# Ordering every engine's stream by hand in an attention + ReGLU-FFN kernel on one core

## The chip, the cores and the metric

The kernel runs on one core of one Trainium2 chip. The metric is device time in microseconds (us), taken as the median of several executions; lower is better. A profile of one execution is there for every kernel. Its span, from the first to the last instruction, is about 2 us shorter than the device time (420.0 against 421.8 for the kernel before), so differences are what is compared between the two.

The engines are called as in the profile: PE (TensorE, matmuls), PEld (its weight loads), DVE (VectorE), ACT (ScalarE), POOL (GpSimd), SP (SyncE, which here only issues DMAs). "L214" is line 214 of a kernel; the two kernels have different line numbers for the same code.

## The reference

Causal attention by blocks of 64, then a gated FFN on the concatenated heads:

```python
# q, k, v: (8, 8, 576, 64) fp32, normal * 0.1   -> B, H, S, D
scores = (1 / sqrt(64)) * (q @ k^T)                 # (B, H, 576, 576)
scores = where(pos // 64 >= pos' // 64, scores, -1e9)
attn   = softmax(scores)                            # (+1e-9 in the denominator)
x      = (attn @ v).transpose(0, 2, 1, 3).reshape(4608, 512)
gate   = max(x @ w_gate, 0)                         # w_gate, w_val: (512, 1536)
out    = (gate * (x @ w_val)) @ w_out               # w_out: (1536, 512), out fp32
```

## The kernel before

The work is cut into 32 head pairs, r = 4 b + hp: four pairs for each of the 8 batches. A pair needs scores (q k^T), an exp on ACT, zeros written over the 64x64 blocks that the mask removes from the diagonal ("corner memsets"), two attention-value products (one for each head), a division by the row sum, and a transpose of the result into xT. The FFN of batch b needs the xT of all four of its pairs. FFN matmuls come out of one generator, and `ffn(n)` emits the next n of them between the steps of the attention of later batches, so that PE has something to do while ACT and DVE work on the attention.

Only PE was ordered by hand. On the other engines a scheduler chose the order. The parts that the change touches (cut):

```python
    def new_stage(w):                       # fp32 landing buffers: 5, used over again
        return sb.tile([128, 2048], FP, name="stage", bufs=5)[:, 0:w]

    def early_load(b, per, gate=None):      # batches 0, 1, 2: load fp32, cast on DVE
        ...
            for t in range(2):
                nc.vector.tensor_copy(m[t][:, :, 64 * h0 : 64 * h1]..., sts[t]...)   # L125
        ...
    def load_batch(b):                      # batches 3 to 7: casting loads on POOL's queue,
        for t, src in enumerate((q, k, v)): # each followed at once by its transposing DMA
            ...                             #   nc.gpsimd.dma_start(dst, src...)       L162
            if t < 2:
                nc.sync.dma_start_transpose(qTm or kTm, m[t])                        # L167
                nc.sync.dma_start_transpose(qTt or kTt, tl[t])

    def scores_1(r):
        sc = scores(b, hp, [(0, 0, True)])
        nc.scalar.activation(at[:, :, 0:512], sc, AF.Exp, scale=scale)
        nc.vector.memset(at[64:128, :, 0:64], 0.0)          # a corner
        sc = scores(b, hp, [(0, 1, True), (384, 3, True)])
        nc.scalar.activation(at[:, :, 512:1024], sc, AF.Exp, scale=scale)
        nc.vector.memset(...); nc.vector.memset(...)        # two more corners
    ...
    with tc.manual_schedule(engines={mybir.EngineType.PE}):
        pe_transposes(0, 0, *early[0])
        for r in range(4):                  # batch 0: nothing to overlap with
            scores_1(r)
            if r < 3:
                pe_transposes(0, r + 1, *early[0])
            if r > 0:
                head_av(r - 1, 0)
            scores_2(r)
            ...
        *early[1], marks1 = early_load(1, 4, w_in)     # waits until the last weight landed
        ...
        ffn(76)
        for r in range(4, 4 * B):
            b, hp = divmod(r, 4)
            a = {1: [2, 2, 4, 6], 2: [4, 4, 4, 12]}.get(b, [8, 4, 8, 16])
            ...
            scores_1(r)
            ffn(a[0])
            if r > 4:
                head_av(r - 1, 0)
                ffn(a[1])
                head_av(r - 1, 1)
                to_xT_pe(r - 1) if r <= 8 else to_xT_dma(r - 1)   # shortened
            ...
            elif hp == 0 and b + 1 < B:
                load_batch(b + 1)
            ffn(a[2])
            scores_2(r)
            scores_3(r)
            ...
            ffn(a[3])
```

The whole kernel before:

The softmax here doesn't subtract the row's maximum and nothing guards it: scores larger than these inputs give would overflow.

## Time and profile before

The median is 421.8 us beside the changed kernel (421.29 to 423.13, 4 runs). What matters, by stretch of the profiled 420.0 us:

| stretch | us | what limits it |
|---|---|---|
| batch 0, up to the first FFN matmul | 0 to 47.7 | serial chain of one pair's attention, at a half-speed PE |
| rest of FFN 0, batch 1, batch 2 (pairs 4 to 11) | 47.7 to 137.7 | mixture: PE busy 67.3 of the 80 us from 60 to 140 |
| batches 3 to 7 | 137.7 to 339 | PE, 40.25 us a batch |
| last pair's end and last FFN parts | to 420 | PE |

From the page of the kernel before: the span, busy tenths of PE in 40 slices of 10.5 us each, the granted PE clock in tenths of full speed, and the shares of the chain of waits.

```profile
span 420.0 us, 7452 instructions
...
PE   2672796887899999999999999999999999999995
...
PEclk9955599999999999999999999999999999999999
...
PE 75%; DMA 7%; DVE 6%; issue 5%; ACT 4%; SPq 2%; POOL 1%; ACTq 0%; DVEq 0%
```

PE is at 9 tenths or more from the 12th slice on and has holes before it; slices 1 and 4 are the worst. The chain of waits, too, runs through PE for 75% of the span. What is to be gained by order therefore lies at the front.

The table by stretch of the kernel before. Its columns are the stretch, its length, then busy us (and instruction counts) of PE, PEld, DVE, ACT and POOL, the granted clock, the mean share of DMA engines in use and GB/s.

```profile
60.00:140.00 80.00, 67.31 (x637) 33.55 (x647) 46.91 (x132) 35.95 (x51) 29.33 (x35) 1.00 1.46 134
140.00:340.00 200.00, 195.80 (x1654) 93.78 (x1684) 88.87 (x241) 93.06 (x139) 33.54 (x40) 1.00 0.76 88
```

In 200 us of steady batches PE stands for 4.2 us, so that 0.84 us of a 40.25 us batch is not PE work.

The timeline of PE before: start, duration, engine, line, operation, result<-operands, tile shapes, count, and in brackets the idle time before the instruction with what ended it.

```profile
4.13 0.61 PE L195 MATMUL ffnp<-ident,q_bf 128*128 128x128 bf16 x4 [4.13 <-DVE q_bf L125]
...
42.20 0.61 PE L293 MATMUL ffnp<-ident,xnat 128*128 128x128 bf16 x4 [8.18 <-DVE xnat L276]
...
47.66 1.49 PE L316 MATMUL ffnp<-xT,wg_75 128*128 128x512 bf16 x3 [0.33 <-issue]
...
68.89 0.40 PE L195 MATMUL ffnp<-ident,k_bf 128*128 128x128 bf16 x4
```

Two things are to be seen. Four 128-wide transposes take 0.61 us at 4 and at 42 us and 0.40 at 69 us: PE runs cold at the front. And PE stands for 8.18 us before 42.20, waiting for a division on DVE. The timeline of DVE says what DVE did in that time:

```profile
39.30 0.69 DVE L125 CAST q_bf<-stage 128x1024 bf16<-128x1024 f32 x1 [6.25 <-DMA stage<-in_q_dram]
...
41.66 0.48 DVE L276 TENSOR_TENSOR xnat<-av,recip 128x320 bf16<-128x320 f32 x1
```

It had been given a cast of batch 1 to do first, and stood 6.25 us for the data of it. The PE part of the table of waits before (total us, times, longest) has this as its largest line:

```profile
PE ffnp L293 <- DVE xnat L276: 13.9, 8, 8.2
```

### The profile page before, as it was taken

The page shows a single profiled execution, that of the slowest core. Times are in us where ns is not written, and L with a number is a line of the kernel's source. Part 1 is how long each engine was busy: PE and PEld are TensorE (multiplying, and loading weights), DVE is VectorE, ACT ScalarE, POOL GpSimd, SP SyncE. Part 2 cuts the span into 40 slices and gives each one's busy share as a digit, 9 for nine tenths or more (in the row PEclk, how much of TensorE's full clock was granted, in tenths as well). Part 3 has the DMA queues.
Part 4 walks back from the last instruction along what each step waited for, and adds up shares of the span by engine and source line. Part 5 has one row for each costly group of instructions (what it writes and reads, how often), then busy time and mean ns, then how long its engine had stood idle before and what let it go on. Part 6 is the DMA issues. An engine that isn't in the chain of part 4 may idle for free.

```text
span 420.0 us, 7452 instructions
## 1 busy us (share of the span) xinstructions
PE 373.0 (89%) x2941; PEld 181.5 (43%) x2992; DVE 192.9 (46%) x503; ACT 161.7 (39%) x237; POOL 73.4 (17%) x98
## 2 busy tenths in 40 slices
PE   2672796887899999999999999999999999999995
PEld 1441443444444444444444444444444444444442
DVE  4742456755565444443444444444434442433331
ACT  1532033443445435544553455245425521321320
POOL 2500200034737370065003000300000000000000
PEclk9955599999999999999999999999999999999999
DMA  8998989239999999299539304920021002002004
GB/s 205 186 203 181 232 149 275 36 47 167 166 126 124 146 195 112 44 149 188 63 71 130 112 16 83 164 68 14 16 91 48 19 19 100 0 2 100 2 1 99
DMA packets 144274, 43.54 MB, mean 104 GB/s; under 512 B 127856, under 2 KB 139632, under 8 KB 144240
## 3 DMA queue, kind: packets, MB, share of 16 engines
q0 software_dynamic: 76128, 13.57, 48.2%
q1 hardware_dynamic: 68112, 29.51, 32.5%
q8 instruction: 23, 0.38, 0.4%
q14 instruction: 11, 0.09, 0.1%
HBM read 37.75 MB, written 9.44 MB: 112 GB/s over the span
## 4 chain that ended last, share of the span: by engine, by line
PE 75%; DMA 7%; DVE 6%; issue 5%; ACT 4%; SPq 2%; POOL 1%; ACTq 0%; DVEq 0%
PE ffnp L344 22%; PE ffnp L328 20%; PE ffnp L316 19%; PE av L266 6%; PE sc L214 6%; DMA wv_82<-in_moe_w_val_dram 3%; DVE xnat L276 2%; DMA stage<-in_v_dram 2%; DMA stage<-in_k_dram 1%; PE ffnp L195 1%; ACT attnT_95 L232 1%; ACT gate_sb L325 1%; ACT attnT_95 L229 1%; DVE recip L275 1%; SPq L133 1%
## 5 line engine op out<-in xcount | busy, mean ns | idle before, releaser
L325 ACT ACTIVATE gate_sb<-ffnp 128x512 bf16<-128x512 f32 x108 | 64.5, 597 | 136.6 <-PE ffnp L316 134.3
L338 DVE TENSOR_TENSOR hT<-gate_sb,ffnp 128x512 bf16<-128x512 bf16 x108 | 74.3, 688 | 70.7 <-PE ffnp L328 68.9
L344 PEld LDWEIGHTS <-hT 128*128 128x128 bf16 x432 | 39.1, 98 | 43.5 <-issue 1.7
L354 DVE COPY ob<-ffnp 128x512 f32<-128x512 f32 x36 | 24.9, 692 | 56.5 <-PE ffnp L344 53.8
L344 PE MATMUL ffnp<-wo_84,hT 128*128 128x512 bf16 x141 | 36.6, 379 | 0.2
L344 PE MATMUL ffnp<-wo_85,hT 128*128 128x512 bf16 x138 | 36.1, 380 | 0.4
L344 PE MATMUL ffnp<-wo_83,hT 128*128 128x512 bf16 x136 | 35.8, 380 | 0.4
L276 DVE TENSOR_TENSOR xnat<-av,recip 128x320 bf16<-128x320 f32 x64 | 31.5, 491 | 2.2
L162 POOL DMA_DIRECT2D q_bf<-in_q_dram x20 | 17.6, 894 | 82.9 <-PE ffnp L198 44.9
L240 ACT ACTIVATE attnT_95<-sc 128x1024 bf16<-128x1024 f32 x16 | 16.4, 1022 | 33.0 <-PE sc L214 33.0
L240 ACT ACTIVATE attnT_94<-sc 128x1024 bf16<-128x1024 f32 x16 | 16.4, 1024 | 31.5 <-PE sc L214 31.5
L316 PE MATMUL ffnp<-xT,wg_77 128*128 128x512 bf16 x95 | 24.6, 380 | 2.2 <-DVE hT L338 2.1
L266 PEld LDWEIGHTS <-attnT_94 128*128 128x128 bf16 x480 | 18.5, 101 | 18.5 <-DVE xnat L276 14.8
L316 PE MATMUL ffnp<-xT,wg_75 128*128 128x512 bf16 x94 | 25.6, 394 | 0.4 <-issue 0.3
L328 PE MATMUL ffnp<-xT,wv_79 128*128 128x512 bf16 x90 | 25.3, 391 | 0.3
L316 PE MATMUL ffnp<-xT,wg_78 128*128 128x512 bf16 x96 | 24.8, 379 | 0.4 <-DVE qTt_91 L203 0.4
L266 PEld LDWEIGHTS <-attnT_95 128*128 128x128 bf16 x480 | 18.8, 102 | 14.5 <-DVE xnat L276 11.0
L328 PE MATMUL ffnp<-xT,wv_82 128*128 128x512 bf16 x87 | 24.2, 380 | 0.6 <-issue 0.2
L229 ACT ACTIVATE attnT_95<-sc 128x1024 bf16<-128x1024 f32 x16 | 16.4, 1023 | 21.7 <-PE sc L214 21.7
L316 PE MATMUL ffnp<-xT,wg_76 128*128 128x512 bf16 x94 | 24.6, 380 | 0.1
L328 PE MATMUL ffnp<-xT,wv_81 128*128 128x512 bf16 x89 | 24.4, 380 | 0.4
L328 PE MATMUL ffnp<-xT,wv_80 128*128 128x512 bf16 x91 | 24.4, 379 | 0.3
(109 smaller groups left out, 433.5 us busy)
## 6 DMA issues: line engine op xcount, KB each, us to landing
out_dram<-ob SPq DMA_DIRECT2D x32, 256.0 KB, 2.8
stage<-in_v_dram SPq DMA_DIRECT2D x27, 128.0 KB, 4.9
q_bf<-in_q_dram POOLq DMA_DIRECT2D x20, 128.0 KB, 5.8
k_bf<-in_k_dram POOLq DMA_DIRECT2D x20, 128.0 KB, 7.2
stage<-in_q_dram SPq DMA_DIRECT2D x4, 512.0 KB, 4.4
stage<-in_k_dram SPq DMA_DIRECT2D x4, 512.0 KB, 5.5
v_bf_97<-in_v_dram POOLq DMA_DIRECT2D x12, 128.0 KB, 8.0
stage<-in_q_dram SPq DMA_DIRECT2D x4, 256.0 KB, 3.6
```

The lines of the kernel that those rows point to most:

```text
L162: nc.gpsimd.dma_start(dst, src[b, :, 128 * c : 128 * c + n, :].rearrange("h p d -> p h d"),)
L214: nc.tensor.matmul(o, kTm[b % 2][ps, c, hp, :] if c < 4 else kTt[b % 2][ps, hp : hp + 2, :].rearrange("p h n -> p (h n)"), qTm[b % 2][ps, ...
L229: nc.scalar.activation(at[:, :, 0:512], sc, AF.Exp, scale=scale)
L240: nc.scalar.activation(at[:, :, 1024:1536], sc, AF.Exp, scale=scale)
L266: nc.tensor.matmul(av[:, p, :], at[:, hh, col : col + 128], vb[:, c, h, :], start=(p == 0), stop=(c == p), skip_group_check=True,)
L276: nc.vector.tensor_tensor(out=xnat[:, :, 64 * hh : 64 * hh + 64], in0=av[:, :, 0:64], in1=recip.to_broadcast([128, NCH, 64]), op=AX.mult,)
L316: nc.tensor.matmul(gate, wg[i][:, c, fo : fo + 128], x[:, c, :], start=(c == 0), stop=(c == 3),)
L325: nc.scalar.activation(gate_sb, gate, AF.Relu)
L328: nc.tensor.matmul(val, wv[i][:, c, fo : fo + 128], x[:, c, :], start=(c == 0), stop=(c == 3),)
L338: nc.vector.tensor_tensor(out=h, in0=gate_sb, in1=val, op=AX.mult)
L344: nc.tensor.matmul(op, hT[f][:, 128 * s : 128 * (s + 1)], wo[f // 4][:, f % 4, :], start=(f == 0), stop=(f == 11),)
L354: nc.vector.tensor_copy(ob, op)
```

## The change

The intent: take order away from the scheduler on all five engines. Nothing is meant to be computed differently. (1) Landing buffers become ten of half the size, so that no load of batch 0 has to wait until a cast frees one; its casts are spread over DVE, ACT and POOL. (2) Junk matmuls on zeros warm PE and keep it warm. (3) The casts of batch 1 move behind 64 FFN matmuls. (4) Corner memsets move out of the score functions to one place per pair, after the pair's last FFN group, and the second exp goes behind an FFN group; the sizes of the groups change. (5) Since SP is now in program order, the loads of batch b+1 (on POOL's queue) and their transposing DMAs are emitted apart: loads at the first pair of a batch, transposes at the third. Besides, copies of transposed outputs go from DVE to ACT, in batch 0 the second head gets another buffer in PSUM (the memory that matmuls write to), and some memsets of the start go to POOL. The core of the diff (cut, and in parts shortened):

```diff
     def new_stage(w):
-        return sb.tile([128, 2048], FP, name="stage", bufs=5)[:, 0:w]
+        return sb.tile([128, 1024], FP, name="stage", bufs=10)[:, 0:w]
 ...
+    def dma_transposes(b):          # was inside load_batch, right behind the loads
+        for t in range(2):
+            nc.sync.dma_start_transpose((qTm, kTm)[t][b % 2]..., m[t]...)      # L189
+            nc.sync.dma_start_transpose((qTt, kTt)[t][b % 2][:, 0:4, :], tl[t])
 ...
     def scores_1(r):
         nc.scalar.activation(at[:, :, 0:512], sc, AF.Exp, scale=scale)
-        nc.vector.memset(at[64:128, :, 0:64], 0.0)
         sc = scores(b, hp, [(0, 1, True), (384, 3, True)])
-        nc.scalar.activation(at[:, :, 512:1024], sc, AF.Exp, scale=scale)
-        nc.vector.memset(at[64:128, :, 512:576], 0.0)
-        nc.vector.memset(at[64:128, :, 896:960], 0.0)
+        return lambda: nc.scalar.activation(at[:, :, 512:1024], sc, AF.Exp, scale=scale)
 ...
+    def corners(r, eng):
+        for c in (0, 512, 896, 1024):
+            eng.memset(at[64:128, :, c : c + 64], 0.0)
 ...
-        av = psum_av.tile([128, NCH, 65], FP, name="av")
+        if b == 0 and hh == 1:
+            av = psum_ffn.tile([128, NCH, 65], FP, name="ffnp")
+        else:
+            av = psum_av.tile([128, NCH, 65], FP, name="av")
 ...
-        nc.vector.tensor_copy(xT_of(b)[:, hp, :], br[:, 0:512])
+        nc.scalar.copy(xT_of(b)[:, hp, :], br[:, 0:512])
 ...
+    def junk(n):
+        jp = psum_ffn.tile([128, 512], FP, name="ffnp")
+        for _ in range(n):
+            nc.tensor.matmul(jp, ident, zeros, start=True, stop=True)
 ...
-    with tc.manual_schedule(engines={mybir.EngineType.PE}):
+    with tc.manual_schedule(engines={E.PE, E.DVE, E.Activation, E.Pool, E.SP}):
+        ... e0.load(h0) for batch 0; junk(12); casts and transposes of the first heads
         for r in range(4):
-            scores_1(r)
+            scores_1(r)()
             if r < 3:
-                pe_transposes(0, r + 1, *early[0])
+                pe_transposes(0, r + 1, e0.m, e0.tl, (dve, dve))
             if r > 0:
+                corners(r - 1, nc.vector)
                 head_av(r - 1, 0)
+            ... casts of later heads on DVE; junk(2)
             scores_2(r)
 ...
+            junk(2)
+        e1.load(0, w_in[2])
+        e1.load(4)
+        corners(3, nc.vector)
         head_av(3, 0)
         head_av(3, 1)
+        junk(4)
         to_xT_pe(3)
-        *early[1], marks1 = early_load(1, 4, w_in)
-        ffn(76)
+        ffn(64)
+        e1.cast_qk(0, (dve, dve))
+        e1.cast_v(0, pool); e1.cast_v(4, pool)
+        ffn(8)
+        pe_transposes(1, 0, e1.m, e1.tl, (dve, dve))
+        ...; ffn(4)
         for r in range(4, 4 * B):
-            a = {1: [2, 2, 4, 6], 2: [4, 4, 4, 12]}.get(b, [8, 4, 8, 16])
+            a = {1: [2, 6, 2, 4], 2: [4, 8, 4, 8]}.get(b, [4, 8, 8, 16])
+            if r == 8:
+                for h0 in (0, 4):
+                    e2.cast_qk(h0, (dve, dve))
-            scores_1(r)
+            exp_2 = scores_1(r)
             ffn(a[0])
+            exp_2()
 ...
-            elif hp == 0 and b + 1 < B:
-                load_batch(b + 1)
+            if hp == 0 and 2 <= b < B - 1:
+                load_qkv(b + 1, (0, 1, 2))
+            if hp == 2 and 2 <= b < B - 1:
+                dma_transposes(b + 1)
             ffn(a[2])
             scores_2(r)
             scores_3(r)
 ...
             ffn(a[3])
+            corners(r, nc.vector)
```

## The prediction

> **What bounds it now.** The chain of waits gives 61% of the 420.0 us span to the three FFN matmul lines. From 140 to 340 us the table by stretch shows PE busy 9.4 to 9.95 us of every 10, and a batch takes 40.25 us there: 144 FFN matmuls at 0.216 us (31.1) plus about 9.0 of attention. The change can gain almost nothing there. The loss is at the front: the first FFN matmul starts at 47.7 us, and from 60 to 140 us PE is busy 67.3 of 80.
>
> In the timeline the front shows four things. (1) PE runs at half rate until about 52 us: four 128-wide transposes take 0.61 us at 4 us and 0.40 at 68 us, 15 attention-value matmuls 1.00 against 0.62, four FFN matmuls 1.71 at 49 us against 0.86. The granted-clock row says 1.0 before 20 us; I trust the durations. The Trainium skill ("TensorE: Matmul & The Clock Gate", Part 1) says a cold array runs at half rate and warms after about 3.4 us of sustained work. (2) A head pair of batch 0 takes about 8 us, serial: the second head waits 2.0 us for the one attention-value buffer, which waits for DVE, which waits for an exp in front of a corner memset. (3) From 33.0 to 41.7 us DVE stands behind casts of batch 1, whose loads wait until the last input weight lands (35.3 us): PE idles 8.2 us. The same happens at 62.8 us (2.1 us). (4) Batch 1 takes 8.9 us a pair, against about 6.7 us of warm PE work.
>
> **What the change does.** Junk matmuls (12 x 0.43 us cold, ending near 7 us, when the tails of q and k land anyway) warm PE; two or four more keep it warm, 0.43 us each pair of them. ACT, Pool and a second PSUM buffer take work off the serial chain; DVE remains at about 5 us a pair (evacuations 1.75, head outputs 1.4, casts 1.3, memsets 0.45), warm PE with junk 4.2. Batch 0 needs no buffer twice, but its 3.5 MB still arrive at about 200 GB/s, so the last quarter lands at 16 to 20 us; weights now compete with it. The casts of batch 1 move behind 64 FFN matmuls.
>
> **Sum.** First scores 8.6 us (9.6 before); four pairs at about 5 us; 3 us to the last transpose: FFN starts at about 32 us, 15 to 16 earlier, all on the critical path. Warm PE work from there: 352 us (1296 FFN matmuls 279.7, 28 pairs at 2.25, transposes 9); tail 3 us. Stalls that stay: 5 us in batch 1 (the transpose of each output still directly follows its last matmul, about 1 us each), 1.5 in batch 2, 1.5 later, 2 where DVE waits for batch 1's second half (loads are DMA-bound: 16.5 MB landed by about 60 us before, and that total doesn't shrink). 32 + 352 + 3 + 10 = **397 us**, range 388 to 409. Chances: faster by over 2% 0.93, within 2% 0.05, slower 0.02.
>
> **Right or wrong by:** first FFN matmul at 28 to 37 us; transposes of four at 0.40 us from about 8 us on; no DVE cast wait over 3 us between 25 and 45 us; a batch-1 pair at 7.5 to 8 us; batches 3 to 7 unchanged at 40.1 to 40.3 us; last FFN stretch unchanged.
>
> **What would break it:** PE turning cold again while DVE, in strict order, stands behind a cast of late data (first FFN at 40 us or more, total near 408); weights starving batch 0's last loads; batch 1's second half landing after 52 us; SP, now strictly ordered, holding output stores behind a load or transpose.

## More of the kernel before

SP's timeline before, where the transposing DMAs of batch 3's q and k (first needed by PE at 137.7 us) are issued; SPq marks SP's issue time:

```profile
99.76 4.02 SPq L167 DMA_TRANSPOSE qTm_87<-q_bf  x1
...
105.25 1.74 SPq L167 DMA_TRANSPOSE kTm_89<-k_bf  x1
```

## The result, and the profile after

The changed kernel takes 408.53 us (406.82 to 409.17, 4 runs) against 421.81 before. The ratio is 0.9674, with a 95% interval of 0.9636 to 0.9713: faster by 3.3%. The prediction's central value was 397 us: the gain is about half of the one foretold, and the time lies at the upper edge of the range.

The same lines of the page after (slices of 10.2 us):

```profile
span 406.5 us, 7570 instructions
...
PE   6789898879964999999999999999999999999995
...
PEclk9989989999995999999999999999999999999998
```

The holes at the front are smaller. But there is a new one: slices 12 and 13 (from about 112 to 132 us) show 6 and 4 tenths, where the kernel before has 9, and the granted clock in slice 13 is 0.5.

Reading the start of each pair's first score matmul from the two timelines gives where the 13.4 us of span came from (419.96 and 406.52 before rounding):

| from, to | before, us | after, us | difference |
|---|---|---|---|
| start to first scores | 9.58 | 7.78 | −1.8 |
| first scores to first scores of pair 3 | 20.43 | 18.64 | −1.8 |
| those to the first FFN matmul | 17.65 | 6.68 | −11.0 |
| to first scores of batch 1 | 22.78 | 19.94 | −2.8 |
| batch 1 (pairs 4 to 7) | 30.78 | 29.18 | −1.6 |
| batch 2 (pairs 8 to 11) | 36.51 | 45.08 | **+8.6** |
| batch 3 (pairs 12 to 15) | 40.26 | 40.90 | +0.6 |
| pairs 16 to 30 | 150.54 | 147.11 | −3.4 |
| pair 31 to the end | 91.43 | 91.21 | −0.2 |

The front gave 17.4 us up to the start of batch 1, and batch 2 lost 8.6 of it. The timeline of PE after:

```profile
33.10 1.12 PE L345 MATMUL ffnp<-xT,wg_75 128*128 128x512 bf16 x4
...
127.30 1.03 PE L236 MATMUL sc<-qTm_87,kTm_89 64*128 64x512 bf16 x6 [9.03 <-DMA kTm_89<-k_bf]
128.26 1.89 PE L357 MATMUL ffnp<-xT,wv_82 128*128 128x512 bf16 x4
```

The first FFN matmul comes at 33.10 us instead of 47.66. At 127.30 PE has stood 9.03 us, for the transposed k of batch 3, and the matmuls after it run at half speed (1.89 us for four where 1.03 is usual): PE came out of the wait cold. The table of waits has it as its largest line; the 13.9 us behind DVE's division have shrunk to 4.0:

```profile
PE sc L236 <- DMA kTm_89<-k_bf: 9.0, 1, 9.0
PE ffnp L322 <- DVE xnat L305: 4.0, 5, 0.9
```

SP's timeline after, and POOL's (where a DMA_DIRECT2D is a casting load being written to the queue), show what happened to these DMAs:

```profile
107.59 1.21 SPq L330 DMA_TRANSPOSE xT<-xnat  x1
...
110.31 3.80 SPq L189 DMA_TRANSPOSE qTm_87<-q_bf  x1
...
115.65 5.91 SPq L189 DMA_TRANSPOSE kTm_89<-k_bf  x1
```

```profile
108.45 3.50 POOL L179 DMA_DIRECT2D q_bf<-in_q_dram  x4 [15.95 <-PE ffnp L220]
...
112.60 3.54 POOL L179 DMA_DIRECT2D k_bf<-in_k_dram  x4
```

Batch 3's transposes now go at 110.3 and 115.7 us instead of 99.8 and 105.3, although the changed kernel is ahead by then. They are emitted at the third pair of batch 2 (pair 10) and stand in SP's program order behind the transposes of pair 9's output (107.59). The data had been there for long: the trace has the last load of batch 3's q and k landed at 86.1 us. They fall onto the loads of batch 4, which POOL could issue from 108.45 on, when the last PE transposes of batch 2 had given their buffers free. The issue of the k transpose takes 5.91 us, and the DMA view of 105 to 130 us after (last column: us from issue to landing) says that the data came late too:

```profile
qTm_87<-q_bf SPq DMA_TRANSPOSE x1, 9.7
...
kTm_89<-k_bf SPq DMA_TRANSPOSE x1, 11.6
```

Last, the steady batches, in the table by stretch after:

```profile
168.00:315.00 147.00, 147.00 (x1261) 71.67 (x1260) 64.60 (x180) 70.91 (x104) 29.35 (x35) 1.00 0.80 97
```

PE has no gap here (in the same stretch before it was busy for 143.78 of 147 us), and a batch takes 39.24 us instead of 40.25.

### The profile page after: what moved, and what is told of

The parts are those of the page before. It is cut to its first block, busy times and chain, and to the rows that moved or that the text cites. A ratio compares the mean times of both kernels' runs of the same rounds, so it can differ in the third digit from the quotient of the medians.

```text
span 406.5 us, 7570 instructions
## 1 busy us (share of the span) xinstructions
PE 376.4 (93%) x3024; PEld 183.0 (45%) x3024; DVE 178.9 (44%) x468; ACT 169.1 (42%) x257; POOL 83.2 (20%) x114
## 3 DMA queue, kind: packets, MB, share of 16 engines
q1 hardware_dynamic: 68112, 29.51, 32.5%
## 4 chain that ended last, share of the span: by engine, by line
PE 83%; DVE 7%; DMA 4%; issue 1%; SPq 1%; ACT 1%; POOL 1%; DVEq 0%; ACTq 0%
PE ffnp L357 23%; PE ffnp L373 22%; PE ffnp L345 22%; PE sc L236 7%; PE av L295 7%; DMA kTm_89<-k_bf 3%; DVE xnat L305 1%; DVE qTm_86 L221 1%; DMA stage<-in_k_dram 1%; PE ffnp L217 1%; DVE hT L367 1%; PE ffnp L322 1%; DVE k_bf L145 1%; DVE q_bf L145 1%; DMA k_bf<-in_k_dram 1%
## 5 line engine op out<-in xcount | busy, mean ns | idle before, releaser
L373 PE MATMUL ffnp<-wo_85,hT 128*128 128x512 bf16 x144 | 37.4, 380 | 0.0
L373 PE MATMUL ffnp<-wo_84,hT 128*128 128x512 bf16 x144 | 37.3, 379 | 0.0
L373 PE MATMUL ffnp<-wo_83,hT 128*128 128x512 bf16 x144 | 37.2, 380 | 0.0
L261 ACT ACTIVATE attnT_95<-sc 128x1024 bf16<-128x1024 f32 x16 | 16.4, 1026 | 35.6 <-PE sc L236 31.6
L305 DVE TENSOR_TENSOR xnat<-av,recip 128x320 bf16<-128x320 f32 x60 | 29.5, 492 | 2.1
L251 ACT ACTIVATE attnT_94<-sc 128x1024 bf16<-128x1024 f32 x16 | 16.4, 1025 | 32.8 <-PE sc L236 24.4
L357 PE MATMUL ffnp<-xT,wv_82 128*128 128x512 bf16 x96 | 26.6, 400 | 0.0
L261 ACT ACTIVATE attnT_94<-sc 128x1024 bf16<-128x1024 f32 x16 | 16.4, 1024 | 23.9 <-PE sc L236 23.9
L251 ACT ACTIVATE attnT_95<-sc 128x1024 bf16<-128x1024 f32 x16 | 16.4, 1025 | 23.2 <-PE sc L236 22.0
L345 PE MATMUL ffnp<-xT,wg_78 128*128 128x512 bf16 x96 | 25.2, 383 | 0.3 <-DVE hT L367 0.3
L357 PE MATMUL ffnp<-xT,wv_81 128*128 128x512 bf16 x96 | 24.7, 380 | 0.4 <-DVE qTt_90 L225 0.4
L357 PE MATMUL ffnp<-xT,wv_79 128*128 128x512 bf16 x96 | 24.7, 380 | 0.4 <-DVE qTt_90 L225 0.4
L357 PE MATMUL ffnp<-xT,wv_80 128*128 128x512 bf16 x96 | 24.7, 379 | 0.4 <-DVE qTt_90 L225 0.4
L345 PE MATMUL ffnp<-xT,wg_75 128*128 128x512 bf16 x96 | 24.8, 379 | 0.0
L179 POOL DMA_DIRECT2D v_bf_97<-in_v_dram x15 | 12.6, 856 | 59.5 <-PE av L295 53.1
L345 PE MATMUL ffnp<-xT,wg_76 128*128 128x512 bf16 x96 | 24.7, 380 | 0.0
L345 PE MATMUL ffnp<-xT,wg_77 128*128 128x512 bf16 x96 | 24.7, 380 | 0.0
L295 PEld LDWEIGHTS <-attnT_95 128*128 128x128 bf16 x480 | 19.4, 101 | 10.6 <-DVE xnat L305 2.1
```

The costliest lines, as they stand in the source:

```text
L179: nc.gpsimd.dma_start(dst, src[b, :, 128 * c : 128 * c + n, :].rearrange("h p d -> p h d"),)
L261: nc.scalar.activation(at[:, :, 1024:1536], sc, AF.Exp, scale=scale)
L295: nc.tensor.matmul(av[:, p, :], at[:, hh, col : col + 128], vb[:, c, h, :], start=(p == 0), stop=(c == p), skip_group_check=True,)
L305: nc.vector.tensor_tensor(out=xnat[:, :, 64 * hh : 64 * hh + 64], in0=av[:, :, 0:64], in1=recip.to_broadcast([128, NCH, 64]), op=AX.mult,)
L345: nc.tensor.matmul(gate, wg[i][:, c, fo : fo + 128], x[:, c, :], start=(c == 0), stop=(c == 3),)
L357: nc.tensor.matmul(val, wv[i][:, c, fo : fo + 128], x[:, c, :], start=(c == 0), stop=(c == 3),)
```

## The experiments

Twelve kernels ran, all with outputs that the comparison with the reference accepts. Those of one round stand beside the same runs of the kernel before: tr_early, no_collide, no_junk and casts_early; exp2_now, a_old, front_dve and fix; stage5, best1 and best2; both_old alone. no_collide, no_junk and casts_early are edits of the changed kernel, the others also hold the edit of tr_early. The stretches (columns four to seven) are read from one profiled execution of each. The edits are shown cut to their core.

| run | median us (range) | ratio to before, 95% interval | first FFN matmul, us | batch 1 | batch 2 | steady batch |
|---|---|---|---|---|---|---|
| before | 421.8 | 1 | 47.66 | 30.78 | 36.51 | 40.25 |
| the change | 408.53 (406.8–409.2) | 0.9674 (.9636–.9713) | 33.10 | 29.18 | 45.08 | 39.24 |
| tr_early | 397.91 (396.5–398.0) | 0.9412 (.9387–.9438) | 34.90 | 27.89 | 37.24 | 39.24 |
| no_collide | 398.26 (397.1–400.2) | 0.9433 (.9397–.9469) | 32.45 | 27.89 | 37.36 | 39.23 |
| no_junk | 410.76 (410.0–412.1) | 0.9719 (.9692–.9745) | 35.71 | 27.89 | 46.85 | 39.24 |
| casts_early | 423.28 (422.4–424.7) | 1.0024 (.9994–1.0055) | 50.08 | 27.89 | 46.79 | 39.24 |
| exp2_now | 407.95 (406.3–410.1) | 0.9658 (.9608–.9708) | 33.55 | 28.52 | 38.04 | 40.66 |
| a_old | 405.59 (403.9–406.2) | 0.9588 (.9551–.9626) | 33.01 | 31.28 | 38.68 | 39.97 |
| front_dve | 397.02 (396.3–398.4) | 0.9400 (.937–.943) | 36.63 | 27.89 | 35.91 | 39.23 |
| fix | 397.47 (395.7–397.7) | 0.9398 (.9367–.9428) | 33.39 | 29.62 | 34.73 | 39.24 |
| stage5 | 398.74 (397.1–400.0) | 0.9424 (.9389–.946) | 33.08 | 28.53 | 37.15 | 39.24 |
| best1 | 393.38 (392.9–394.6) | 0.9304 (.9283–.9325) | 30.69 | 30.59 | 34.74 | 39.24 |
| best2 | 391.66 (391.5–392.8) | 0.9265 (.9246–.9285) | 30.81 | 27.78 | 34.74 | 39.24 |
| both_old | 416.35 (416.0–416.7) | 0.9861 (.9829–.9893) | 33.58 | 29.83 | 42.57 | 41.47 |

### tr_early and no_collide: where the missing 11 us went

Theory: batch 3's transposes are too late and collide with batch 4's loads. Rivals: they are late only because of their place in SP's order; or the data of batch 3 itself landed late; or the collision alone does it. One run moves the transposes one pair earlier; the other leaves them where they are and holds batch 4's loads back behind them.

```diff
# tr_early
-            if hp == 2 and 2 <= b < B - 1:
+            if hp == (1 if b == 2 else 2) and 2 <= b < B - 1:
                 dma_transposes(b + 1)
# no_collide: first POOL load of batch 4 depends on the last transposing DMA of batch 3
-                load_qkv(b + 1, (0, 1, 2))
+                load_qkv(b + 1, (0, 1, 2), tr3 if b == 3 else None)
```

> The four transposing DMAs of batch 3 (q, q tail, k, k tail) are issued one head pair earlier (r=9 instead of r=10), nothing else. My theory: in the changed kernel PE stood 9.0 us (118.3 to 127.3) before batch 3's first scores for the k transpose, and ran cold for some 2.5 us after it, only because SP, now in program order, sends these transposes after pair 9's output transpose, so late that they meet the Pool loads of batch 4. Then the wait is gone, the stretch from the first scores of batch 2 to those of batch 3 falls from 45.1 to about 36 us or less, and the total is 396 to 399 us. Rival (loads of batch 3 themselves late, or the four DMAs slow wherever they stand): they still land after 118 us or end 10 us after their issue, a wait of over 4 us stays, total 403 us or more.

> The transposing DMAs of batch 3 stay where the change put them (r=10), but the Pool loads of batch 4 now wait until the last of them has landed. If the collision with those loads is what stretches the transposes (q 3.8 us and k 5.9 us of issue, 11.6 us to landing, against about 2.0 and 4.7 elsewhere), issue falls to about 2 us each, k lands near 119 us, and 6 to 8 us of the 9.0 us wait go: total 399 to 402 us. If the lateness of the issue alone makes the wait, the transposes keep their length and the total stays at 406 to 409 us. The loads of batch 4 come some 10 us later; I expect that to cost nothing, since they are needed at about 148 us.

Both take the whole loss away: 397.91 and 398.26 us, against 408.53. SP's timeline and the score matmuls in PE's timeline with tr_early (their line has no bracket: PE doesn't wait for them at all):

```profile
102.71 2.12 SPq L189 DMA_TRANSPOSE qTm<-q_bf  x1
...
106.57 2.95 SPq L189 DMA_TRANSPOSE kTm<-k_bf  x1
```

```profile
118.71 0.61 PE L236 MATMUL sc<-qTm,kTm 64*128 64x512 bf16 x6
```

With no_collide the k transpose is issued at 113.19, only 2.5 us earlier than in the changed kernel. SP's issue and PE's wait, and the DMA view of 105 to 130 us:

```profile
113.19 2.02 SPq L191 DMA_TRANSPOSE kTm<-k_bf  x1
```

```profile
117.65 0.61 PE L241 MATMUL sc<-qTm,kTm 64*128 64x512 bf16 x6 [0.31 <-DMA kTm<-k_bf]
```

```profile
qTm<-q_bf SPq DMA_TRANSPOSE x1, 4.3
...
kTm<-k_bf SPq DMA_TRANSPOSE x1, 4.4
```

Issue falls from 5.91 to 2.02 us and landing from 11.6 to 4.4 us by nothing but the absence of the loads, and PE waits 0.31 us instead of 9.03. So both conditions were needed. The late place alone costs 0.3 us. The collision alone costs nothing if it comes early enough: in tr_early, too, POOL's first load of batch 4 begins at 107.67, and the k transpose takes 7.5 us to land, but it lands at 114.0, and PE asks for it at 118.71. That the data had landed late is ruled out by the landing at 86.1 us, 24 us before the transposes were issued. The Trainium skill says ("DMA: Bandwidth & Descriptors", "Queues, rings and completion order") that each DMA engine takes turns between the queues that it has work for, a packet at a time. The stretching agrees with that; how much a transpose loses by it, the page doesn't say, and here it was a factor of about 2.6 to landing.

The kernel before had the sign of it in its trace. Its q transpose, issued at 99.76 among casting loads, took 4.02 us, the k transpose at 105.25, in a gap of theirs, 1.74. There PE did not need them until 137.7.

### no_junk: what the junk matmuls are worth

```diff
     def junk(n):
-        for _ in range(n):
+        for _ in range(0):
             nc.tensor.matmul(jp, ident, zeros, start=True, stop=True)
```

> All junk matmuls of the changed kernel taken out. My theory: they keep PE warm, so without them it is cold from the start until about 36 us: transposes of four at 0.61 us, 15 attention-value matmuls at 1.0 us. The first FFN matmul then comes 1 to 4 us later than 33.1 us (the junk's own time, about 7 us of PE work, is saved, but every real matmul of the front takes twice as long), the FFN's first 3 us run cold, total 2 to 5 us over the changed kernel. Rival: PE isn't what bounds the front (DVE and arriving data are), and junk in front of real work costs as much as it brings: first FFN matmul within 1 us of 33.1 or earlier, total within 2 us.

The FFN starts at 35.71 us instead of 33.10, and the whole kernel takes 2.2 us more (410.76; the four runs of each do not overlap, but the intervals of the two ratios just do). PE's timeline and the table by stretch without junk:

```profile
35.01 0.61 PE L322 MATMUL ffnp<-ident,xnat 128*128 128x128 bf16 x4 [0.81 <-DVE xnat L305]
...
35.71 1.89 PE L345 MATMUL ffnp<-xT,wg 128*128 128x512 bf16 x4
```

```profile
20.00:30.00 10.00, 8.29 (x99) 5.51 (x99) 4.43 (x19) 6.22 (x10) 1.48 (x2) 1.00 1.31 203
```

The transposes take 0.61 us right up to the FFN, so PE was cold for the whole front, which the granted clock of 1.00 in the table denies: durations are the safer reading here. So the junk does what it was put in for, but it isn't what moved the start of the FFN from 47.7 to 33.1; about 2.6 us of 14.6 are its share, read from one profile of each, where equal fronts differ by up to 2.5 us (below). It isn't fully reliable either. In the runs with junk PE still fell back for a time, at a different place each time. In tr_early, for instance, the table by stretch has a clock of 0.63 from 10 to 20 us (the 8.5 us busy count the slowed matmuls at their full length):

```profile
10.00:20.00 10.00, 8.54 (x84) 4.75 (x84) 6.50 (x20) 4.41 (x6) 7.42 (x10) 0.63 1.25 251
```

Between kernels whose fronts are the same the start of the FFN varies from 32.5 to 34.9 us, tr_early's being the latest.

### casts_early: is the place of batch 1's casts the main gain?

```diff
         e1.load(4)
+        e1.cast_qk(0, (dve, dve))
         corners(3, nc.vector)
 ...
         ffn(64)
-        e1.cast_qk(0, (dve, dve))
```

> One part undone: the casts of batch 1's first half go back ahead of the end of batch 0's attention in DVE's order, as they stood before the change. My theory: DVE's strict order behind late data was the main loss of the front, so DVE again stands until these loads land (issue at 28.5 to 34 us, landing 34 to 40 us), the first FFN matmul moves from 33.1 to 39 to 43 us, and the total grows by 4 to 9 us (the DVE burst at 48 us with its PE gap of 1.7 us and some 2 us of cold time goes away in return). Rival: the front's gain came from the shorter chain per pair, buffers and warm PE: the first FFN matmul moves by less than 3 us.

It is, and by more than the text above allows (4 to 9 us): 423.28 us, no faster than the kernel before, and 14.7 us more than the changed kernel. The timelines of DVE and PE with the casts back in front:

```profile
37.99 0.69 DVE L145 CAST q_bf<-stage 128x1024 bf16<-128x1024 f32 x1 [7.77 <-DMA stage<-in_q_dram]
42.22 0.69 DVE L145 CAST k_bf<-stage 128x1024 bf16<-128x1024 f32 x1 [3.53 <-DMA stage<-in_k_dram]
```

```profile
46.01 1.01 PE L295 MATMUL av<-v_bf,attnT 128*128 128x65 bf16 x15 [15.21 <-DVE attnT L275]
```

DVE stands for four loads in turn (7.77, 3.53, 1.66 and 0.37 us), the corner memsets of pair 3 stand behind the casts, and PE stands 15.21 us behind the memsets. The FFN starts at 50.08 us. The wait exceeds the 8.18 us of the kernel before by 7.0 us. 3.2 of them come from PE being there earlier (it starts to wait at 30.80 us instead of 34.02), 3.8 from its going on later (46.01 instead of 42.20): the scheduler had slipped a memset and a division in between the casts (at 40.06 and 41.66 us), where the strict order keeps the memsets that PE waits for behind all four. The loads don't come sooner for a faster front: those of batch 1's first q and k land at 38 to 45 us here and at 38 to 46 in the changed kernel, where DVE doesn't wait for them. With this one placement undone, all the rest of the change, its loss in batch 2 included, comes to nothing. (It shows the size of this wait in the new order; how the scheduler's own order would have fared with the rest of the new front was not run.)

### front_dve and stage5: the parts of the front that moved nothing

front_dve undoes the use of ACT for casts and copies and the second PSUM buffer in batch 0, on top of tr_early; stage5 gives batch 0 a ring of five landing buffers that it must use over again.

```diff
# front_dve
-        e0.cast_qk(0, (dve, act)); pe_transposes(0, 0, e0.m, e0.tl, (dve, act))
+        e0.cast_qk(0, (dve, dve)); pe_transposes(0, 0, e0.m, e0.tl, (dve, dve))
-        nc.scalar.copy(xT_of(b)[:, hp, :], br[:, 0:512])
+        nc.vector.tensor_copy(xT_of(b)[:, hp, :], br[:, 0:512])
-        if b == 0 and hh == 1:
+        if False:
# stage5
-        return sb.tile([128, 1024], FP, name="stage", bufs=10)[:, 0:w]
+        nm = "stage0" if batch0 else "stage"
+        return sb.tile([128, 1024], FP, name=nm, bufs=5 if batch0 else 10)[:, 0:w]
```

> On top of tr_early: in batch 0 the work given to ACT goes back to DVE (k cast, k evacuation, the copies of the transposed outputs of the first nine pairs) and both heads share the one attention-value buffer again; Pool keeps its two v casts, since they also hold back the weight loads. My estimate from the traces: the second head waits about 1.2 us a pair (reciprocal 0.20, multiply 0.49, hand-overs) and DVE does 0.8 us more a pair, so the first FFN matmul comes 3 to 6 us later than the 34.9 us of tr_early and the total grows by 3 to 7 us, the rest in batch 1. Rival: the front is bound by arriving data and by the exps on ACT, which gets lighter: less than 2 us.

> On top of tr_early: batch 0 gets its own staging ring of 5 buffers of the same size, so its loads have to reuse buffers (11 of them are wanted in turn; the others keep their ring of 10). If staging without reuse is what brings batch 0's data in time, the loads of its second half are issued 1 to 4 us later (each waits for a cast), the pairs r=2 and r=3 start later and the first FFN matmul moves by 1 to 3 us beyond the 33.0 to 34.9 us seen so far, total +1 to +3 us. If the arrival rate bounds them anyway, the first FFN matmul stays within 33 to 35 us and the total within 1.5 us.

Neither can be told from tr_early in the total (397.02 and 398.74 us against 397.91, with overlapping intervals); for front_dve 3 to 7 us had been expected. front_dve starts the FFN 1.7 us later, which is within what equal fronts differ by, and has most of it back by batch 2, which takes 35.91 instead of 37.24 us. In stage5 the last loads of batch 0's v are issued at 11.82 us instead of about 11.1, and it changes nothing after that: in the new order a ring of five hardly holds the loads up. Staging batch 0 without reuse, and ACT's part of its casts and copies, have no gain that these runs can show. (POOL's two casts of v stayed in all of them, and what reuse cost with the order of the kernel before was not run.)

### exp2_now, a_old, both_old: the steady batches

The prediction had batches 3 to 7 unchanged at 40.1 to 40.3 us; they take 39.24. Two moves of the change can do that, the second exp behind an FFN group and the new sizes of the groups. They are undone one at a time and together, on top of tr_early.

```diff
# exp2_now
-            exp_2 = scores_1(r)
-            ffn(a[0])
-            exp_2()
+            scores_1(r)()
+            ffn(a[0])
# a_old
-            a = {1: [2, 6, 2, 4], 2: [4, 8, 4, 8]}.get(b, [4, 8, 8, 16])
+            a = {1: [2, 2, 4, 6], 2: [4, 4, 4, 12]}.get(b, [8, 4, 8, 16])
# both_old: both of these
```

> On top of tr_early: the second exp of each pair goes back to directly behind the first, ahead of the FFN group's ReLU (its place before the change). My theory: the 1.0 us that every steady batch gained (40.25 to 39.24 us) comes from the ReLU no longer standing behind two exps of 1.0 us, so a batch goes back towards 40.2 us and the total grows by 4 to 6 us (five full batches and some in batches 1 and 2). Rival: the gain comes from the other split of FFN matmuls round the attention, or from the moved corner memsets: a batch stays at 39.2 to 39.4 us.

> On top of tr_early: the FFN group sizes of the kernel before ([2,2,4,6], [4,4,4,12], [8,4,8,16]) in place of the new ones, all else as changed. If the split is what gains in the steady batches, a batch goes back to about 40.2 us (total +5 us or more); if the exp placement does it, it stays at 39.2 to 39.5. In batches 1 and 2 fewer FFN matmuls stand between the two heads (2 and 4 for 6 and 8), so the second head waits for the one attention-value buffer, about 0.9 us a pair: I expect those two batches together 3 to 6 us longer.

> On top of tr_early: both the second exp behind the first and the old FFN group sizes, the last corner of the square whose other corners are tr_early (39.24 us a steady batch), exp2_now (40.66) and a_old (39.97). If the two moves add up, 41.4 us a batch; if these two are all that separates the steady batches of before and after, it comes back to the 40.25 us of the kernel before, so that the moved corner memsets and the order of the other engines give nothing there. If it stays below 40.1, some of the gain is theirs. Total between 404 and 412 us.

| us per steady batch | new group sizes | old group sizes |
|---|---|---|
| second exp behind the group | 39.24 (tr_early) | 39.97 (a_old) |
| second exp at once | 40.66 (exp2_now) | 41.47 (both_old) |

The two effects add: 1.42 and 0.73, and 2.23 together. Much of this was not foretold: exp2_now was expected 4 to 6 us slower and near 40.2 us a batch, a_old at either 40.2 or 39.2 to 39.5, both_old at 404 to 412 us in all; only both_old's 41.4 us a batch, for effects that add, was met. In the whole kernel the exp's place is worth 8 to 10 us (8.4 between the profiled runs, 407.95 against 397.91 in the medians), nearly as much as the collision, and it has nothing to do with the front. The mechanism can be read in exp2_now, in the timelines of ACT, DVE and PE:

```profile
201.46 1.02 ACT L251 ACTIVATE attnT<-sc 128x1024 bf16<-128x1024 f32 x1 [1.51 <-PE sc L236]
202.38 1.02 ACT L253 ACTIVATE attnT<-sc 128x1024 bf16<-128x1024 f32 x1
203.28 1.27 ACT L354 ACTIVATE gate_sb<-ffnp 128x512 bf16<-128x512 f32 x2
```

```profile
203.92 0.69 DVE L367 TENSOR_TENSOR hT<-gate_sb,ffnp 128x512 bf16<-128x512 bf16 x1 [2.51 <-PE ffnp L345]
```

```profile
205.29 0.64 PE L295 MATMUL av<-v_bf,attnT 128*128 128x65 bf16 x15 [0.33 <-DVE xnat L305]
```

ACT does both exps (about 1 us each) and only then the ReLU of an FFN block that PE had long finished. DVE, in order, stands 2.51 us before it can multiply gate and value. (Its line names PE's L345, but these are matmuls of the next block, which the multiplication doesn't read; it begins at 203.92, and the ReLU that it does read ends at 203.88.) The division of the first head stands behind the multiplication, and the second head's matmuls stand behind the division. That this is the whole cost shows when the PE matmuls of one batch (pairs 20 to 23) are laid beside those of tr_early, which stand in the same order: all 1.41 us arise in two of the four pairs, each time 0.2 us at the value matmuls in front of the second head and 0.5 us at the second head. In the changed kernel the ReLU lies between the two exps:

```profile
188.28 1.02 ACT L251 ACTIVATE attnT_94<-sc 128x1024 bf16<-128x1024 f32 x1 [1.45 <-DVE attnT_95 L275]
189.21 0.59 ACT L354 ACTIVATE gate_sb<-ffnp 128x512 bf16<-128x512 f32 x1
189.68 1.03 ACT L253 ACTIVATE attnT_94<-sc 128x1024 bf16<-128x1024 f32 x1
```

There is a second thing in the table. both_old has the exps and group sizes of the kernel before, and still takes 41.47 us a batch against its 40.25. The rest of the hand order therefore costs about 1.2 us a batch; the two placements win that back and 1.0 more. Which part of it costs this is not settled. It may be the corner memsets at the end of a pair instead of behind each exp, or the generator, which emits a ReLU only when the next `ffn` call resumes it, so that in program order it falls behind exps that were emitted after its matmuls. The trace of both_old has such a case (the exps of scores at 163.61 and 164.53, the ReLU at 164.69), and the kernel before shows the scheduler's choice, the ReLU at 174.17 ahead of the exp at 174.66. That is a reading, not a test: no run separates the two.

### fix: a fault in the changed kernel

Reading the timelines turned up that the changed kernel isn't right. PE transposes q of batch 2's first pair at the end of pair 7, but the cast that writes it is emitted at pair 8. From the timelines of PE and DVE after:

```profile
80.21 0.40 PE L217 MATMUL ffnp<-ident,q_bf 128*128 128x128 bf16 x4
```

```profile
83.33 0.69 DVE L145 CAST q_bf<-stage 128x1024 bf16<-128x1024 f32 x1
```

The transpose reads the buffer 3 us before it is written, and finds q and k of batch 0 there, since two buffers take turns. Heads 0 and 1 of batch 2 get their attention weights from the wrong batch. The comparison doesn't notice: with inputs of 0.1 the scores are so small that the softmax is nearly flat, and putting batch 0's q and k for those two heads into the reference moves the whole output by 0.36% (relative L2), about 1% within batch 2. A check for races has nothing to find, because in program order it is no race: the write simply comes after the read. The kernel before doesn't have the fault; of the runs here all but fix, best1 and best2 have it. The mend casts batch 2 at pairs 6 and 7:

```diff
-            if r == 8:
-                for h0 in (0, 4):
-                    e2.cast_qk(h0, (dve, dve))
+            if r in (6, 7):
+                e2.cast_qk(4 * (r - 6), (dve, dve))
```

> A correction on top of tr_early. The changed kernel casts batch 2's q and k at r=8, but PE transposes batch 2's first pair at r=7, before the cast is written: that pair's scores come from batch 0's q and k, still in the same buffer. The outputs pass because the scores are tiny (computed apart: 0.36% of the whole output's norm). Here the two casts stand at the start of r=6 and r=7. I expect a correct result and, since DVE no longer has 3 us of casts in one block at r=8 (PE waited 1.2 us there for the first head's output and more behind it), the stretch from the scores of r=8 to those of r=9 falls from 12.8 us to 9.5 to 11.5, and the total by 0 to 3 us. If the data of batch 2 is not there at r=6, DVE stalls and the total rises.

It takes 397.47 us, the same as tr_early. The casts no longer hold up pair 8 (pair 8 takes 10.29 us instead of 12.80) and hold up batch 1 instead: it takes 1.7 us longer, 1.1 of them at pairs 6 and 7, where the casts stand; the other 0.6 lies at pair 4, in front of them, where PE has a cold spell (four FFN matmuls at 52.03 us took 1.86). The gain of the change is not owed to the fault.

### best1 and best2: a version that beats both

Both are right where the changed kernel is not, and put together what the runs above taught: transposes early; in batch 0 the corner memsets of a pair come ahead of the evacuations (the copies out of PSUM) of the next pair's transposes on DVE; in batch 1 the transpose of a pair's output waits until the next pair's last scores, so that it no longer follows directly on the division that it needs.

```diff
# both, on top of tr_early
             scores_1(r)()
+            # batch 0
             if r > 0:
-                corners(r - 1, nc.vector)     # ahead of head_av, behind the evacuations
                 head_av(r - 1, 0)
+            # corners(r - 1, nc.vector) now directly behind scores_1(r)()
 ...
-                if r <= 8:
+                if r == 8:
                     to_xT_pe(r - 1)
 ...
             scores_3(r)
+            if 4 < r < 8:
+                to_xT_pe(r - 1)
# best1: batch 2's casts on DVE as in fix, batch 1's casts 8 FFN matmuls earlier
# best2: batch 2's casts on POOL, emitted at pair 4
-                    e2.cast_qk(h0, (dve, dve))
+                    e2.cast_qk(h0, (pool, pool))
```

> On top of fix, three placements that its trace asks for: in batch 0 the corner memsets of a pair stand ahead of the next pair's evacuations on DVE (PE waited 1.0 to 1.3 us three times for them); in batch 1 the transposes of a pair's output come after the next scores instead of right behind its last matmul (PE waited 0.8 to 0.9 us each, three of the four can move); the casts of batch 1's first half stand 8 FFN matmuls earlier. I expect 2 to 3 us at the front, 2 us in batch 1, 0 to 2 from the casts: total 392 to 395 us against 397.5 for fix. If DVE is the bound there, the waits move to the next instruction and less than 1.5 us comes.

> As best1, but batch 1's casts stay where they are and the casts of batch 2's q and k go to Pool, in data order, instead of DVE at r=6 and r=7. If the DVE casts at r=6 and r=7 cost the 1.7 us that batch 1 lost in fix against tr_early, this gets them back: 391 to 394 us. Rival: Pool and DVE slow each other (a DVE cast took 1.54 us instead of 0.69 beside a Pool cast in the changed kernel), and it is no faster than best1.

best2 is the fastest kernel: 391.66 us, ratio 0.9265 to the kernel before, 4% below the changed one. Which of its placements gives how much was not run one by one. From its page:

```profile
PE   7799998889999999999999999999999999999995
```

The FFN starts at 30.81 us, batch 2 takes 34.74, and from the 10th slice on PE is at 9 tenths or more until the last. best1 needs 30.59 us for batch 1 where best2 needs 27.78; it was 0.9 us ahead at the start of batch 1, and 2.0 us behind at the end. Two things make the difference, and no run parts them. At pairs 6 and 7, where batch 2's casts stand on DVE, best1 loses 1.4 us. As much, 1.45 us, it loses at pair 4, through its earlier casts of batch 1: they bring DVE to those of the second half before the data is there (it stands 1.76 and 0.89 us for q and k at 50.44 and 52.02), and PE stands 1.49 us behind. Casts on POOL are not free for DVE, though. In the changed kernel DVE's cast of k for batch 1, begun at 48.48 us, took 1.54 us instead of 0.69, beside a cast on POOL that had begun at 48.40 (1.07 us). The Trainium skill says ("SBUF — State Buffer", "SBUF: two separate sides") that the two engines share a pair of ports as an exclusive lock: when DVE's instruction is in a mode that uses both of its ports, the one that comes second is blocked for the whole instruction. 0.99 us left of POOL's cast and 0.69 for its own make an estimate of 1.68, 0.14 more than is measured; the mode itself the trace doesn't show. In best2 the casts of batch 2 therefore went where DVE has no casts to do.

## Why the prediction was right or wrong

**Direction and front: right.** It foretold a first FFN matmul at about 32 us (28 to 37); it came at 33.10. The terms were less exact: the sum had a pair at about 5 us, and three pairs took 18.64 us, 6.2 each; an earlier start (7.78 for 8.6) and a shorter end made up for part of it. It foretold that DVE would stand for no cast over 3 us between 25 and 45 us, and none does (the first cast of batch 1 begins at 47.88, without a wait). It named the casts of batch 1 as what broke the front; casts_early shows that this is the largest single part, 14.7 us in the new order.

**The step that failed: "Stalls that stay: ... 1.5 in batch 2".** The wait at the start of batch 3's scores was 9.03 us, and the cold PE behind it cost 1.7 us more (pair 12 took 11.47 instead of 9.80); tr_early, without them, takes 397.91 us. Taking them away takes away 10.6 of the 11.5 us between 397 and 408.5. What would break the prediction did name "SP, now strictly ordered", but the wrong way round: it had output stores held behind a load or transpose, and what happened was an input transpose held behind output transposes, then stretched by loads. It could have been asked beforehand, if not costed. The order of the new SP stream is in the diff, the trace of before has a q transpose of 4.02 us among loads, and POOL's loads start when batch 2's last PE transposes free their buffers. What I didn't ask was which transfers the new order would put side by side.

**"batches 3 to 7 unchanged at 40.1 to 40.3 us": wrong, in our favour.** They take 39.24. I read "PE busy 9.4 to 9.95 us of every 10" as "the change can gain almost nothing there". It was about 0.84 us a batch of PE gaps, and more was to be won and lost: 2.2 us a batch between the best and the worst of the four combinations of exp place and group sizes.

**The agreement of 397 with tr_early's 397.9 is partly luck.** My sum has 32 us to the FFN and 365 from there; in spans, tr_early has 34.90 and 361.3. A front too optimistic by 2.9 us and a rest too pessimistic by 3.7, where the steady batches alone came out about 1 us each below the forecast, nearly cancel.

**"Batch 1 takes 8.9 us a pair": a misreading.** Pairs 4 to 7 took 30.78 us in the kernel before, 7.7 a pair; I had taken a window that reached into batch 2. So the "7.5 to 8 us" foretold as an improvement was no improvement; 7.3 was measured.

**Junk: right in kind.** "0.40 us from about 8 us on" held for the transposes of the changed kernel's front (0.39 or 0.40 from 5.76 us on), but PE fell back between them: at 21.97 us 15 attention-value matmuls took 1.01 us, the cold duration. Its worth is 2.2 us in the total, which the prediction had not set apart. The Trainium skill ("TensorE: Matmul & The Clock Gate", Part 1) says that the array warms after about 3.4 us of sustained work and that the window in which this is judged runs freely, so the moment varies. The traces agree: in the changed kernel twelve junk matmuls from 1.79 us on took 4.13 us, which is about seven at the cold 0.43 and five at the warm 0.216, so PE was warm after about 3 us; in front_dve they took 5.19, all cold.

**Batch 0 without reuse, spread casts: nothing measurable.** The prediction said that batch 0's loads are bound by bandwidth and that only its serial chain gets shorter; front_dve shows that what ACT and the second PSUM buffer take off that chain is within the noise of the total, and stage5 that the buffers are.

## What to carry to other kernels

When an engine or a queue is put into program order, write down for each DMA it issues the time by which it is needed and what else will be in the queues then: a transfer that was harmless early can be both late and slow a few microseconds on. Never put an instruction that waits for a load in front of work that something critical waits for on the same in-order engine; here one such place (casts_early) cost as much as the whole change gained. And a full-looking engine is worth a second look, since the place of one exp against a ReLU made 1.4 us of every 39.

## What the Trainium skill lacked or had wrong

- "DMA: Bandwidth & Descriptors" says that engines take turns between queues, and in its rules, where they are about corrupted data, that a transpose next to ordinary DMAs "needs nothing". It doesn't say what that costs in time. Beside casting loads from POOL's queue a transpose took 11.6 us to land instead of 4.4 and 5.9 us to issue instead of 2.0. No page gives such a figure.
- "TensorE: Matmul & The Clock Gate", Part 1, has PE go cold after an idle window of about 3.4 us. In tr_early it went cold between 12 and 14 us, though from 6 us on it had never stood for more than 1.2 us at once; it had been busy for 2.0 of the 4 us from 6 to 10. The page speaks of frequent short stops in another kernel, too, but doesn't tell how busy is busy enough.
- The same page warns that the clock events can't be fully trusted, which the runs bear out, if the profile's granted clock comes from them: without junk it reads 1.00 for the first 40 us, while four 128-wide transposes took 0.61 us, the cold duration, up to 35 us.
- "GPSIMD Engine Reference", section 3.1, gives 769 ns for 512 elements as measured in the best case, about 1.8 cycles an element, and in the same paragraph 1.03 cycles for short loop bodies. POOL's cast of 128x512 from fp32 to bf16 took 0.62 us in the changed kernel (at 7.64) and that of 128x1024 1.06 (at 54.88, with no cast on DVE beside it): the difference is 0.86 ns an element, an estimate from spans that are rough on POOL, near the 1.03 cycles at the page's 1.2 GHz. For a cast the 769 ns are not the best case.
